# Turned rows by TensorE transposes instead of DMA transposes, and late row pairs folded by VectorE

## The chip, the cores and the metric

The kernel runs on one core of one Trainium2 chip. The metric is the device time of the program in microseconds (us), as the median of several runs; lower is better. Names of engines: PE is TensorE (PEld its weight loads), DVE is VectorE, ACT is ScalarE, POOL is GpSimd, and SP is SyncE, which here only issues DMAs.

## The reference, cut to what matters

Four layers are applied to `x` of 2048 rows by 512 columns, a spectral layer (A) and a mixing MLP (B) in turn, twice, each on the normalised rows and added to `x`:

```python
def _A_ref(x, w_r, w_i):
    X = rfft2(x)
    X = X * (w_r + 1j * w_i)
    return irfft2(X, s=(S, D)).astype(bfloat16)

def _B_ref(x, w1, w2, w3, w4):            # w1, w2: 512x512; w3: 512x1792; w4: 1792x512
    h = _gelu(_layernorm(x) @ w1)
    # quarters of h's columns shifted by +1, -1, +2, -2 rows
    hs = concatenate([g0, g1, g2, g3]) @ w2
    x1 = x + hs
    return x1 + _gelu(_layernorm(x1) @ w3) @ w4

x = A_x
x = x + _A_ref(_layernorm(x), A_w_r, A_w_i)
x = x + _B_ref(_layernorm(x), B_w1, B_w2, B_w3, B_w4)
x = x + _A_ref(_layernorm(x), A_w_r, A_w_i)
x = x + _B_ref(_layernorm(x), B_w1, B_w2, B_w3, B_w4)
```

## The kernel before

The whole state `x_state` stays in SBUF as 128 partitions by 16 row blocks `q` by 512 columns; row `16 p + q` lies in partition `p`. The kernel calls `layer` twice; one `layer` is one spectral layer and the MLP behind it.

The spectral layer is a chain of small matmuls. A Fourier transform over `p` (`front`) gives `V`; then over the columns (`over_d`), over `q` (`over_q`), the product with the filter `W` (`weigh`, which writes `PB`), and back over `q` (`back_q`), over the columns (`back_d`, letters D and C, with the table `G`) and over `p` (`back_p`, letter P, with the table `Tinv`). Between two of them ACT or DVE copies the result out of PSUM. `back_d` of a pair `m` of row blocks leaves two halves in PSUM, an even and an odd part of the columns. `take_D` (letter Y) copies both to SBUF as `Y`, and `back_p` then makes each half of the 512 columns from both parts with two accumulating matmuls: four matmuls of 256 columns for each row block. `half_D` and `fold_D` (letters K and H) are a second way that the code holds: ACT or DVE copies the odd half to SBUF, DVE writes the sum and the difference of the parts as `Y`, and `back_p` then needs only two matmuls. The constant `FOLD` lists for which `m` the second way is taken; before, for none.

In the MLP, rows must be turned before the products with `w1` and `w3`, so that columns lie on the partitions. `norm2` and `norm3` write normalised rows to `xn`, and `turn` turns two row blocks, 128x1024, with one DMA transpose from SP to the tile `xT`: letter T before `w1` (function `tr`), letter U before `w3` (`tr3`); eight of each in a layer. `w1` (letter v) and `w3` (letter w) multiply, `gelu1` (h) and `gelu3` (g) on ACT take the results out; `w2` (letter u), `add_x1` (f), `w4` (letter W) and `add_x2` (A) end the MLP. The statistics of the norms are letters s and k on ACT.

The program is scheduled by hand. Three strings, `ORDER_0` for the first `front`, `ORDER_A` and `ORDER_B` for the two calls of `layer`, name every operation in the order in which it is issued; each engine works through its own operations in that order. A last letter A, V, P or D says which engine does an operation that could run on several, and a number behind a dot says which of the eight PSUM banks it writes:

```python
    for op in (ORDER_B if last else ORDER_A).split():
        op, _, bank = op.partition(".")
        K.bank = int(bank) if bank else None
        if op[0] == "X":
            fill(K, int(op[1:]))
            continue
```

SP's queue carries, in this order: `x`, the filter `W` in four groups (`load_W`), then, after a small copy `gate2` that waits until the last part of `W` is in place, `G`, `Tinv`, `w1`, `w2`, `w3`; a dummy transpose; the transposes, with `w4` issued behind the eighth of the first layer; and at the end the stores. POOL's queue carries the tables `FL`, `TL`, `TR`, and four copies W to W that double the filter. ACT's queue carries the table `T` and one column of each of the two planes of `W`. `fill` issues matmuls on zeros.

Of the kernel before, what the change touches and what calls it, by code (L numbers as in the profile page):

```python
# [13 lines left out]
BF16 = dt.bfloat16  # L14
FP32 = dt.float32

P = 128
# [11 lines left out]
def dft_tables():  # L29
# [12 lines left out]
    p = np.arange(P)  # L42
    pair = lambda j, s: (j if s == 0 else 64 - j) if j else 32 * s
    T = np.zeros((P, NH, 2, 2))
    for j in range(NH):
        for s in range(2):
            i = pair(j, s)
            T[:, j, s, 0] = np.cos(2 * np.pi * i * p / 128)
            T[:, j, s, 1] = np.sin(2 * np.pi * i * p / 128) if i else np.cos(np.pi * p)
    T = T.reshape(P, P)  # L50
    d = np.arange(D // 2)
    f = np.arange(1, 257)
# [9 lines left out]
    w = np.full(256, 2.0)  # L62
    w[255] = 1.0
    G = np.stack([cos * w, sin * w]) / (S * D)
    G = G.transpose(2, 0, 1).reshape(2, P, 2, D // 2).transpose(1, 0, 2, 3)
    A = np.zeros((NH, NQ, 2, 2, 2, 32))
    B = np.zeros((NH, NQ, 2, 2, 2, 32))
    q = np.arange(NQ)
    for j in range(NH):
        for sg in range(2):  # L70
            for m in range(32):
                k = 64 * m + (j if sg == 0 else 64 - j if j else 32)
# [24 lines left out]
           "Tinv": np.stack([T.T, -T.T], axis=1)}  # L97
# [43 lines left out]
def banks(K, n):  # L141

    k = K.bank
    if k is None:
        k = K.next_bank if K.next_bank + n <= 8 else 0
        K.next_bank = (k + n) % 8
    return K.ps[:, k:k + n, :]


def copy(K, dst, src, eng):  # L150
    if eng == "V":
        K.nc.vector.tensor_copy(dst, src)  # L152
    else:
        K.nc.scalar.activation(dst, src, ACT.Copy, bias=0.0, scale=1.0)  # L154


def load_all(K, A_x, A_w_r, A_w_i, B_w1, B_w2, B_w3, B_w4):
# [16 lines left out]
    for pl, v in enumerate(planes):  # L174
        nc.scalar.dma_start(K.W[2::4, pl, 0], v[:, 32])
    for lo in range(0, NH, 8):
        for pl, v in enumerate(planes):
            load_W(K, v, pl, lo, lo + 8)
    K.TL = K.const.tile([P, 2, NB, P], BF16, name="TL")
# [28 lines left out]
    def load_mlp():  # L208
        gate2 = K.const.tile([1, 16], BF16, name="gate2")
        nc.sync.dma_start(gate2[:], K.W[1:2, 1, NH - 1, 1:17])  # L210
        for k in ("G", "Tinv"):
            table(k, nc.sync)
        for k, w, n, c in (("w1", B_w1, 4, D), ("w2", B_w2, 4, D), ("w3", B_w3, 4, FH), ("w4", B_w4, 14, D)):
            t = K.const.tile([P, n, c], BF16, name=k)
            setattr(K, k, t)
            if k != "w4":
                load_halves(t, w, n)

    def load_w4():
        load_halves(K.w4, B_w4, 14)  # L220

    def load_halves(t, w, n):
        v = w.rearrange("(t p) n -> p t n", p=P)
        for part in (slice(0, n // 2), slice(n // 2, n)):
            nc.sync.dma_start(t[:, part], v[:, part])

    K.load_w4 = load_w4
# [10 lines left out]
def load_W(K, v, pl, lo, hi):  # L238


    j1 = max(lo, 1)
    fwd, rev = [K.W[2 * sg::4, pl] for sg in range(2)]
    K.nc.sync.dma_start(fwd[:, lo:hi], v[:, lo:hi])
    K.nc.sync.dma_start(rev[:, j1:hi], v[:, 65 - hi:65 - j1][:, ::-1])
# [243 lines left out]
def first_front(K):  # L488
# [66 lines left out]
    dummy = K.const.tile([P, 1, P], BF16, name="dummy")  # L555
    K.nc.sync.dma_start_transpose(dummy[:], K.zeros[:])
# [11 lines left out]
def layer(K, last):  # L568
# [144 lines left out]
    def turn(to, k, rows):  # L713

        g, h = divmod(k, 2)
        if g not in to:
            to[g] = K.grp.tile([P, 4, 4, P], BF16, name="xT", bufs=4)
        nc.sync.dma_start_transpose(to[g][:, 2 * h:2 * h + 2].rearrange("p q t c -> p (q t) c"),
                                    rows.rearrange("p q d -> p (q d)"))

    def tr(k):
        turn(xT, k, xn[:, 2 * k:2 * k + 2, :])
        turned.append(k)
        if len(turned) == 8 and not last:
            K.load_w4()
# [48 lines left out]
    def tr3(k):  # L774
        q = ROWS[2 * k]
        turn(xT3, k, xn[:, q:q + 2, :])
# [84 lines left out]
    def act_table(k):  # L861
# [4 lines left out]
    next_V, turned = {}, []  # L866
    table = {"z": act_table, "e": lambda g: ln[g].std_twice(), "i": lambda g: ln[g].invert_twice(), "M": lambda g: ln[g].shift(), "J": invert4, "d": over_d, "t": take_d, "q": over_q, "x": take_q, "p": weigh, "b": lambda b: back_q(b, first_half(b)), "V": lambda b: back_q(b, 1),
             "D": lambda m: back_d(m, 0), "C": lambda m: back_d(m, 1), "Y": take_D, "P": back_p, "a": add_x, "s": stats2, "r": rstd2, "c": lambda g: ln[g].ratio(), "n": norm2,
             "T": tr, "v": w1, "h": gelu1, "u": w2, "f": add_x1, "k": square3, "E": resid,
# [34 lines left out]
FLEX = "mlGLnotxYIKEpQ"  # L904
FOLD = [(), ()]
ORDER_0 = """
s1 f0 s0 s3 s2 i3 i2 i0 s4 s5 S1 J1 s7 S0 J0 s6 i7 f2 Q2A Q3A i4 Q0A s9 i6 s8 O1.2 s11 f3 S2 J2 Q6P Q1A Q5A O0.4 i8
G1A Q4V O2.0 s10 i11 i10 S3 Q7P O3.2 G0A s13 J3 Q10V Q11A s12 s14 i12 O5.6 i14 G3A i13 G2A Q8P Q9P s15 S4 J4 O4.4 G5A
i15 Q12V Q13V S5 O6.0 L5A J5 Q14P O7.6 G4A G6A G3V Q15V L6V G7A O8.0 L7A G8A I3V L8A
"""  # L910
ORDER_A = """
d0.3 t0A d2.4 d1.2 d4.0 q0.6 t1V N0 t2A q1.2 d6.4 t4A q2.0 x1V x0V p1V t6A q4.2 d12.6 d10.4 x2A p2P p0V t12A t10A d8.0
p4D b0.6 d14.7 q10.4 m0V q6.2 t8A x10A t14A b1.0 b5.1 m5A m1A q12.4 q14.6 p6D b4.1 b2.0 p10V x14A p14P d15.2 m4A m2A
t15A q8.6 x8A b3.1 b7.0 m7A b11.2 q15.6 m11A x15A b10.3 b14.0 m3A b6.2 m6A p12D V12.4 b12.5 p8V p15V b13.7 b9.1 m10A
m12A b8.6 b15.2 m13V V15.3 m14V m9A m8V V13.5 V14.0 m15A D1.6 l12V D0.1 l15A l13A l14V C1 C0 Y0V Y1A D3.3 C3 P3.0 a3
P2.6 Y3A a2 s3 P0.5 a0 s2 P1.2 a1 s0 D2.0 C2 Y2V s1 r0 D5.6 C5 P7.2 a7 Y5A e0 s7 P6.4 D7.0 P4.5 a6 i0 M0 P5.2 D4.6 C4
P10.3 s6 C7 n2P a4 s4 a5 n3V n0V s5 Y4A D6.4 r1 P11.2 C6 P8.6 P9.7 e1 n1V a10 T1 Y7A P15.0 i1 M1 n5A s10 n4P n6P P14.1
Y6V P13.3 a8 s8 T0 a9 n7P s9 a11 P12.4 a15 s11 v1.6 r2 n10P T2 h1 T3 a13 a12 n11V c0 s15 T5 n8V v0.2 h0 s13 v3.4 n9V
v2.2 h3 u0.0 s12 h2 u1.4 a14 c1 s14 T4 u3.1 r3 f0 k0 n14V v5.2 n13A n15V T7 f1 E1V h5 f3 v4.6 u2.0 f2 E2V h4 c2 u6.6
f6 u5.5 f5 E5V k3 E6V n12P u7.0 E0V u4.1 f4 T6 v7.5 k2 k1 R0 E3V o2V o1V h7 o3A c3 v6.1 h6 o0P f7 u8.0 f8 E8P u13.5  # L920
u12.2 u11.6 u14.3 U1 f12 k4 k5 k7 f14 E14V k12 k6 u9.2 f11 u10.4 k8 E7V f13 k13 f10 R1 o7P o5P u15.3 E10V U0 w4.0 E4P
f9 E9P k11 f15 w2.4 g2 k10 o4V U2 w1.2 k14 g4 E15P k9 E13P w3.6 g3 g1 w5.0 w0.4 g0 w6.6 g5 g6 E11V W1.2 o6P U3 E12V A1
W3.6 A3 B3 B1 w8.0 W2.4 A2 W0.2 k15 R2 o10P o11A R3 o14V o9A g8 o12A w13.0 U5 w7.6 B2 g13 o8P U4 w15.4 w10.0 A0 B0 g10
w16.2 j1 g7 g16 w18.0 g18 w9.2 o15P w11.0 g9 w12.2 g12 j3 w17.6 j2 j0 S0 Q3V Q1V Q2P Q0V g11 W4.2 U7 O1.0 o13P g17 U6
A4 W7.3 B4 j4 G1A G1V A7 B7 j7 O0.0 w19.6 G0A W6.2 A6 g19 W5.3 A5 g15 B5 w23.4 g23 j5 B6 j6 S1 Q4P G0V w27.2 g27 I0V
w14.6 g14 Q5V O2.0 w20.2 w24.6 g20 W10.2 A10 B10 Q7V j10 W8.3 G2A A8 B8 W9.4 A9 B9 Q6V j9 W11.2 A11 w26.4 I1P B11 j11
g24 j8 O3.2 w22.6 S2 Q10P g26 G2V I2P Q11A Q8P g22 w21.0 g21 G3A w25.6 G3V g25 W12.0 A12 B12 j12 Q9P S12 J12 I3P O4.5
G4A Q12A G4V W15.1 A15 I4P B15 j15 W13.2 A13 S15 J15 B13 j13 W14.3 Q15P W24.2 S13 J13 Q13P O5.0 A14 A24 B14 B24 j14
G5A O15.4 G15V O6.2 S14 J14 L15A Q14A O14.4 G6A L6A G14A G5V I5V L14A
"""  # L930
ORDER_B = """
X6.7 d4.4 d15.7 t15A d12.2 t4V d1.0 d0.1 q15.4 t1V q4.6 t12A x15V q1.2 t0A x4A d2.0 p15P p1D q0.4 p0D q12.6 d10.2 t2A
x12A d8.0 q2.4 d6.6 t10A b1.3 p4V b5.2 t8A t6A q8.0 m1A m5A q6.6 p12P p2D x6A q10.3 b0.2 x10A b3.5 b2.6 m2A b4.7 m4A
d14.4 t14A p8D b9.1 m9A b13.0 p6V b12.3 p10V b7.6 m13A m7A m0A b6.4 q14.0 b15.7 b10.6 m3V b8.2 b11.5 m15A p14D b14.7
m12A m8V m14V V12.0 V14.1 V15.3 V13.2 m10A m6A l14V m11A l12A D2.5 l15V l13A D3.0 C3 Y3A C2 D1.2 C1 Y2V Y1A P7.1 a7
P6.0 a6 P4.5 P5.7 P2.2 P3.3 D0.0 s7 a4 s6 C0 a5 D5.4 s4 s5 r1 C5 a3 s3 Y0V D6.6 a2 e1 P0.0 P1.2 i1 a0 a1 Y5A P10.1 M1
n4V n5P D4.4 C4 P11.0 s2 T2 s0 n7V n6V T3 s1 r0 a10 a11 Y4A C6 e0 i0 D7.2 C7 P9.1 Y6A M0 n0P P8.4 Y7A P12.0 s11 n1V T0
a8 s10 P13.5 a9 s9 n3V n2P T1 c0 P15.2 a15 s8 P14.3 a14 s15 r2 n11V v3.1 h3 v2.3 h2 v0.6 h0 n10P T5 v1.2 a13 s13 n8P
h1 u0.4 s14 n9V T4 u3.5 a12 c1 u1.0 s12 r3 f3 u2.7 f1 k1 n14V n15P T7 f0 v5.2 c3 f2 v4.0 n13A h5 u4.3 n12V T6 f4 E3V
k0 h4 E1V u6.7 c2 u7.6 f7 k3 E0V u5.1 k2 R0 E7V E2V o1P o2P f5 E5V k4 v6.5 h6 o0A v7.0 h7 u13.6 o3V U1 u12.4 u15.5 f6  # L940
E6P f13 E13P u14.3 f14 k7 k5 E14V k6 R1 o7A E4V u11.0 f15 f12 k14 k12 u9.2 E15P f9 k13 o6V u8.1 u10.3 f10 E10V f11
E11V k15 U0 w6.4 w4.2 g4 k9 f8 E8V R3 o15A E12V o13V k10 w5.0 w1.2 g5 o12P k11 g1 w2.6 w0.1 g2 o14V g0 k8 R2 o11V o8P
w3.6 U3 g3 o5A U6 U7 w26.0 w21.2 g21 w22.6 g26 w23.2 E9V o9P g6 W0.0 A0 o4V U2 W3.1 W2.0 g23 g22 w25.2 W1.4 g25 w11.2
g11 o10V w27.6 g27 w8.2 g8 U4 w12.6 A3 A1 w24.4 w10.2 A2 w7.0 g10 g24 W12.2 W14.3 y3 y0 A14 A12 w9.4 g9 W13.2 A13 U5
w13.4 g13 y2 w15.2 W15.4 g7 y1 A15 g12 y12 W6.7 g15 A6 w16.0 g16 y13 W5.2 w17.4 g17 w14.0 g14 w20.4 w18.0 y6 y14 g20
g18 W7.6 A7 y7 W4.4 A5 A4 y4 y5 w19.6 g19 y15 W9.1 A9 W8.3 y9 W11.0 A11 y11 W10.5 W20.4 A8 y8 A10 y10 A20 y20
# [31 lines left out]
```

## Time and profile before

| what | value |
|---|---|
| median of 3 runs | 343.75 us (343.66 to 343.83) |
| the profiled execution's own time | 343.63 us |
| its span, first to last instruction | 341.8 us |
| granted TensorE clock | 1.000 |
| PE busy | 334.3 us, 98% of the span |
| PEld, DVE, ACT, POOL busy | 186.8, 163.5, 192.0, 117.5 us |
| DMA transposes xT<-xn | 32, median 3.1 us from issue to landing |

The layout of the span, by the trace: the first `front` matmul starts at 8.2 us, the first `over_d` at 19.0, `back_d` at 36.8, `w1` at 51.2 us, `w3` from 79 us; the second layer's `over_d` starts at about 182 us, `back_d` at 199.4, `w1` at 214.6 and `w3` at about 242 us. The last matmul ends at 339.1 us.

Busy time of PE is a union over matmuls whose ends are modelled: a matmul of 512 columns is shown with 379 ns although the next one starts 216 ns later. What one costs in a stream is therefore read from a run of equal ones: its length divided by its count.

### The profile page before, as it was taken

How to read it: one execution, taken by the hardware profiler on the slowest of the kernel's cores; microseconds unless marked ns; L12 is line 12 of the kernel's file. 1: busy time of each engine (PE TensorE's matmuls, PEld its weight loads, DVE VectorE, ACT ScalarE, POOL GpSimd, SP SyncE). 2: the span in 40 equal slices, each digit the busy share in tenths (PEclk: the TensorE clock that was granted, in tenths of full speed). 3: DMA queues.
4: the chain of work that ended last, by engine and by line, in shares of the span. 5: the costliest groups of instructions: out<-in, count | busy, mean ns of one | idle time of the engine just before them, and what ended most of it. 6: DMA issues, size and time to landing. Idle time of an engine off the chain costs nothing.

```text
span 341.8 us, 5734 instructions
## 1 busy us (share of the span) xinstructions
PE 334.3 (98%) x2184; PEld 186.8 (55%) x2184; DVE 163.5 (48%) x373; ACT 192.0 (56%) x356; POOL 117.5 (34%) x218
## 2 busy tenths in 40 slices
PE   6999999999999999999999999999999999999996
PEld 4878984444444444444467898444444444444443
DVE  4979895659034023535378979456901110200112
ACT  6989899665821542421628979986695132142310
POOL 3795067669633000402432505877722000000000
PEclk9999999999999999999999999999999999999999
DMA  7985936390231100000000003543130500000011
GB/s 261 313 284 197 339 78 117 71 270 19 46 61 31 32 0 0 2 0 0 2 0 2 2 3 64 104 83 61 33 61 0 125 31 0 15 17 32 15 63 46
DMA packets 45340, 24.60 MB, mean 72 GB/s; under 512 B 35153, under 2 KB 42321, under 8 KB 45313
## 3 DMA queue, kind: packets, MB, share of 16 engines
q1 hardware_dynamic: 43824, 19.74, 23.0%
q0 software_dynamic: 1248, 4.40, 3.9%
q8 instruction: 17, 0.28, 0.3%
q10 hardware_dynamic: 240, 0.10, 0.1%
q14 instruction: 11, 0.08, 0.1%
HBM read 11.61 MB, written 2.10 MB: 40 GB/s over the span
## 4 chain that ended last, share of the span: by engine, by line
PE 85%; ACT 8%; DVE 3%; DMA 2%; issue 1%; SPq 0%; ACTq 0%
PE ps L804 28%; PE ps L784 28%; PE ps L749 8%; PE ps L733 6%; PE ps L642 4%; ACT xn L303 3%; PE ps L612 2%; PE ps L594 2%; DVE x_state L698 2%; PE ps L662 2%; DMA x_state<-in_A_x_dram 1%; ACT hT L740 1%; DMA xT<-xn 1%; PE ps L439 1%; PE ps L429 1%
## 5 line engine op out<-in xcount | busy, mean ns | idle before, releaser
L791 ACT ACTIVATE gT<-ps 128x1024 bf16<-128x1024 f32 x56 | 55.7, 1023 | 97.6 <-PE ps L784 95.5
L804 PE MATMUL ps<-w,gT 128*128 128x512 bf16 (+2 forms) x476 | 99.4, 366 | 0.0
L784 PE MATMUL ps<-xT,w 128*128 128x512 bf16 x448 | 99.3, 379 | 0.0
L810 DVE TENSOR_TENSOR x_state<-ps,x_state 128x512 bf16<-128x512 f32 (+2 forms) x34 | 22.1, 659 | 123.4 <-PE ps L804 123.1
L804 PEld LDWEIGHTS <-gT 128*128 128x128 bf16 x476 | 45.4, 98 | 51.4
L784 PEld LDWEIGHTS <-w 128*128 128x128 bf16 x448 | 43.7, 98 | 52.1
L757 DVE SCALAR_TENSOR_TENSOR xn<-xn,ln_c,ps 128x512 bf16<-128x512 bf16 x32 | 23.3, 742 | 16.0 <-PE ps L749 6.3
L733 PE MATMUL ps<-xT,w 128*128 128x512 bf16 x128 | 28.6, 379 | 0.4 <-DMA xT<-xn 0.4
L749 PE MATMUL ps<-w,hT 128*128 128x512 bf16 x128 | 28.8, 379 | 0.1
L326 POOL TENSOR_SCALAR ln_ve<-ln_mv 128x4 f32<-128x4 f32 x11 | 3.0, 271 | 57.7 <-DVE ln_mv L319 57.0
L303 ACT ACTIVATE junk<-xn 128x512 bf16<-128x512 bf16 x32 | 19.8, 623 | 5.0 <-DVE xn L757 5.0
L291 DVE BATCH_NORM_STATS2 ln_st<-x_state 128x6 f32<-128x512 bf16 (+2 forms) x30 | 19.5, 665 | 3.5 <-DMA x_state<-in_A_x_dram 3.0
L698 DVE SCALAR_TENSOR_TENSOR x_state<-ps,x_state 128x512 bf16<-128x512 f32 x32 | 20.6, 684 | 0.9 <-PE ps L690 0.9
L733 PEld LDWEIGHTS <-w 128*128 128x128 bf16 x128 | 12.4, 98 | 15.6 <-DMA xT<-xn 1.0
L749 PEld LDWEIGHTS <-hT 128*128 128x128 bf16 x128 | 12.5, 98 | 15.4 <-ACT hT L740 1.0
L303 ACT ACTIVATE xn<-x_state 128x512 bf16<-128x512 bf16 x32 | 19.9, 626 | 0.8 <-DVE x_state L698 0.8
L740 ACT ACTIVATE hT<-ps 128x512 bf16<-128x512 f32 x32 | 17.6, 600 | 4.6 <-PE ps L733 4.5
L690 PE MATMUL ps<-Y,Tinv 128*128 128x256 bf16 x128 | 15.8, 272 | 0.4 <-DVE Y L152 0.4
L631 POOL TENSOR_TENSOR PB<-X,W 128x2048 bf16<-128x2048 bf16 (+1 forms) x4 | 12.1, 3033 | 11.2 <-DVE X L152 7.3
L154 ACT ACTIVATE TV<-ps 128x1024 bf16<-128x1024 f32 (+1 forms) x17 | 14.6, 895 | 2.4 <-PE ps L594 2.3
L642 PE MATMUL ps<-TR,PB 128*128 128x128 bf16 x256 | 15.9, 219 | 0.0
L662 PE MATMUL ps<-G,hT 128*128 128x256 bf16 x128 | 15.6, 273 | 0.0
(96 smaller groups left out, 414.0 us busy)
## 6 DMA issues: line engine op xcount, KB each, us to landing
w<-in_B_w_dram SPq DMA_DIRECT2D x4, 896.0 KB, 7.0
W<-W POOLq DMA_DIRECT2D x4, 514.0 KB, 5.1
x_state<-in_A_x_dram SPq DMA_DIRECT2D x8, 256.0 KB, 4.9
out_dram<-x_state SPq DMA_DIRECT2D x15, 128.0 KB, 1.8
w<-in_B_w_dram SPq DMA_DIRECT2D x4, 256.0 KB, 4.4
W<-in_A_w_r_dram SPq DMA_DIRECT2D x7, 128.5 KB, 5.4
W<-in_A_w_i_dram SPq DMA_DIRECT2D x7, 128.5 KB, 5.6
TL<-tab_TL POOLq DMA_DIRECT2D x3, 256.0 KB, 5.5
```

What stands on the lines that cost most here:

```text
L303: K.nc.scalar.activation(out, src, ACT.Square, bias=0.0, scale=D ** -0.5, accum_out=self.s[:, i, 1:2])
L642: nc.tensor.matmul(o[:, k0 * P:(k0 + 1) * P], lhsT=pab[u][:, k, 2 * (b - u) + h, f * P:(f + 1) * P], rhs=K.TR[:, k:k + 2, 2 * b + h], star ...
L662: nc.tensor.matmul(o[:, i, e * 256:(e + 1) * 256], lhsT=M[:, F, e, 2 * m + i, :], rhs=K.G[:, F, e, :], start=(F == 0 and e == 0), stop=(F ...
L698: nc.vector.scalar_tensor_tensor(K.x[:, q, :], ps.pop(("P", q)), 1.0, K.x[:, q, :], op0=ALU.mult, op1=ALU.add, accum_out=ln[g].s[:, i, 0:1])
L733: nc.tensor.matmul(o[:, i], lhsT=K.w1[:, t, j * P:(j + 1) * P], rhs=xT[g][:, :, t, :], start=(t == 0), stop=(t == 3))
L740: nc.scalar.activation(hv[:, 2 * h + i, 4 * g:4 * g + 4, PAD:PAD + P], o[:, i].rearrange("p (q c) -> p q c", q=4), ACT.Gelu_apprx_tanh, bi ...
L749: nc.tensor.matmul(o, lhsT=K.hT[:, j, st:st + P], rhs=K.w2[:, j, :], start=(j == 0), stop=(j == 3))
L757: nc.vector.scalar_tensor_tensor(xn[:, q, :], xn[:, q, :], ln[q // 4].c[:, q % 4:q % 4 + 1], ps.pop(("u", n)), op0=ALU.mult, op1=ALU.add, ...
L784: nc.tensor.matmul(o[:, i], lhsT=K.w3[:, c, t * P:(t + 1) * P], rhs=xT3[g][:, :, c, :], start=(c == 0), stop=(c == 3))
L791: nc.scalar.activation(gT[g][:, 2 * j:2 * j + 2, :], ps.pop(("w", k)), ACT.Gelu_apprx_tanh, bias=0.0, scale=1.0)
L804: nc.tensor.matmul(o, lhsT=gT[g][:, t, i * P:(i + 1) * P], rhs=K.w4[:, t, d], start=(t == 0), stop=(t == 13))
L810: nc.vector.tensor_tensor(x, ps.pop(("W", n)), x, op=ALU.add)
```

## The change

Four things are changed together.

1. `turn` no longer issues a DMA transpose. It issues eight TensorE transposes of 128x128 against a unit matrix, into one PSUM bank read as bf16, and a new operation `take_turned` copies the 128x1024 result to `xT` on ACT or DVE (letters Z behind T and F behind U).
2. `FOLD` lists the row pairs 4 to 7 in both layers.
3. Loads: the unit matrix is loaded on SP behind `Tinv`; `w4` is loaded with the other weights, not behind the eighth transpose; the two column loads of `W` go from ACT's queue to SP's, behind the first group of `W`; the dummy transpose goes.
4. All three orders are new.

```diff
-           "Tinv": np.stack([T.T, -T.T], axis=1)}
+           "Tinv": np.stack([T.T, -T.T], axis=1), "unit": np.eye(P)}
...
-    for pl, v in enumerate(planes):
-        nc.scalar.dma_start(K.W[2::4, pl, 0], v[:, 32])
     for lo in range(0, NH, 8):
         for pl, v in enumerate(planes):
             load_W(K, v, pl, lo, lo + 8)
+        if lo == 0:
+            for pl, v in enumerate(planes):
+                nc.sync.dma_start(K.W[2::4, pl, 0], v[:, 32])
...
-        for k in ("G", "Tinv"):
+        for k in ("G", "Tinv", "unit"):
             table(k, nc.sync)
...
-            if k != "w4":
-                load_halves(t, w, n)
+            load_halves(t, w, n)
...
-    dummy = K.const.tile([P, 1, P], BF16, name="dummy")
-    K.nc.sync.dma_start_transpose(dummy[:], K.zeros[:])
...
-    def turn(to, k, rows):
-
-        g, h = divmod(k, 2)
+    def turn(key, rows):
+
+        ps[key] = o = banks(K, 1)[:, 0].bitcast(BF16).rearrange("p (i t c) -> p i t c", i=2, t=4)
+        for i in range(2):
+            for t in range(4):
+                nc.tensor.transpose(o[:, i, t], rows[:, i, t * P:(t + 1) * P], K.unit[:])
+
+    def take_turned(to, key, eng):
+        g, h = divmod(key[1], 2)
         if g not in to:
             to[g] = K.grp.tile([P, 4, 4, P], BF16, name="xT", bufs=4)
-        nc.sync.dma_start_transpose(to[g][:, 2 * h:2 * h + 2].rearrange("p q t c -> p (q t) c"),
-                                    rows.rearrange("p q d -> p (q d)"))
+        copy(K, to[g][:, 2 * h:2 * h + 2], ps.pop(key), eng)
...
-FOLD = [(), ()]
+FOLD = [(4, 5, 6, 7), (4, 5, 6, 7)]
 ORDER_0 = """
-s1 f0 s0 s3 s2 i3 i2 i0 s4 s5 S1 J1 s7 S0 J0 s6 i7 f2 Q2A Q3A i4 Q0A s9 i6 s8 O1.2 s11 f3 S2 J2 Q6P Q1A Q5A O0.4 i8
+s0 s2 s1 f0 s3 i2 s5 f2 i0 S0 i3 S1 s7 J0 s6 Q0A s4 s9 J1 Q1V O0.5 Q2A i6 i4 i7 S2 s10 J2 Q3A s11 f3 Q4A Q5A s8 i11
...
 ORDER_A = """
...
-P10.3 s6 C7 n2P a4 s4 a5 n3V n0V s5 Y4A D6.4 r1 P11.2 C6 P8.6 P9.7 e1 n1V a10 T1 Y7A P15.0 i1 M1 n5A s10 n4P n6P P14.1
-Y6V P13.3 a8 s8 T0 a9 n7P s9 a11 P12.4 a15 s11 v1.6 r2 n10P T2 h1 T3 a13 a12 n11V c0 s15 T5 n8V v0.2 h0 s13 v3.4 n9V
-v2.2 h3 u0.0 s12 h2 u1.4 a14 c1 s14 T4 u3.1 r3 f0 k0 n14V v5.2 n13A n15V T7 f1 E1V h5 f3 v4.6 u2.0 f2 E2V h4 c2 u6.6
+Y2V Y3A P3.1 P2.3 P7.4 a0 s0 a1 s1 P6.0 a3 s3 D5.6 C5 P4.1 a2 s2 K5A P5.5 D4.2 a6 s6 a7 a4 r0 e0 a5 C4 s7 K4A i0 M0
+n2P n3A s4 D6.4 D7.0 C7 n0P H5 H4 n1V s5 T1.6 Z1A r1 e1 P11.7 P8.2 T0.3 a11 i1 M1 n4P a8 Z0A C6 P10.6 P9.7 n6A v1.2 h1
+a9 n5P T2.7 a10 n7P T3.6 s11 v0.2 K6V H6 Z3V P12.6 Z2A v3.4 K7V c1 c0 s9 P13.7 H7 P15.0 P14.1 s10 s8 h3 h0 r2 v2.4 n9P
...
```

By the two programs' instructions, PE gains 256 transposes (8 turns of each kind in each of 2 layers, 8 transposes each) and loses 32 of its 128 matmuls of `back_p`; every other kind of matmul has the same count. ACT and DVE gain 32 copies of 128x1024. SP's queue holds no transpose any more. The six zero matmuls that opened `ORDER_B` (`X6.7`) stand in front of `P10` now (`X6.2`). In the spectral stage the filter products that POOL did in `ORDER_A` and `ORDER_B` (`p2P p14P` and `p15P p12P`) are on DVE.

## The prediction

> **What bounds the kernel now.** I read the share of busy time first, then the slices, the chain in order of time, the groups by form and what PE waited for.
>
> The page, parts 1 and 2 (busy us, share of the span, instructions; then tenths in 40 slices):
>
> ```profile
> PE 334.3 (98%) x2184; PEld 186.8 (55%) x2184; DVE 163.5 (48%) x373; ACT 192.0 (56%) x356; POOL 117.5 (34%) x218
> ...
> PE   6999999999999999999999999999999999999996
> ...
> PEclk9999999999999999999999999999999999999999
> ```
>
> PE is busy in every slice at full clock. But ends of matmuls are modelled, so I need what a matmul costs in an unbroken stream. The chain of what ended last (start, length, work) gives it:
>
> ```profile
> 72.33 6.91 PE ps L749 x32
> 125.43 0.45 PE ps L439 x8
> 199.53 2.62 PE ps L662 x24
> ```
>
> 6.91/32 = 216 ns for 512 columns, 2.62/24 = 109 ns for 256, 0.45/8 = 56 ns for 128. The second row matters most: each of those eight matmuls has its own 128x128 weights and 128 columns, the shape of a turn.
>
> Now the sum over all matmuls of before, counts from the groups by form: 1124 of 512 columns x 0.216 = 242.8; 28 of 384 (three quarters of 0.216, an estimate) 4.6; 392 of 256 x 0.109 = 42.7; 476 of 128 x 0.056 = 26.7; 128 of L612 at about 0.06 (16 took 0.98 in the chain) 7.8; six zero matmuls 0.7. Together 325.3 us. PE runs from the first front matmul at 8.2 us to 339.1 us, 330.9 us. So all of PE's slack after the head is about **5.6 us**, and PE is the bound nearly everywhere. What the waits name of it is small:
>
> ```profile
> PE ps L429 <- ACT Tq L412: 2.4, 2, 1.9
> ...
> PE ps L733 <- DMA xT<-xn: 0.4, 2, 0.3
> PE ps L690 <- DVE Y L152: 0.4, 1, 0.4
> PE ps L588 <- DVE V L471: 0.3, 1, 0.3
> ```
>
> Only 0.4 us of PE's waiting is for a DMA transpose: what the change removes is nearly hidden already.
>
> One stage is tight on three engines, the end of the spectral layer (busy us and counts of PE, PEld, DVE, ACT, POOL, then clock, DMA share, GB/s):
>
> ```profile
> 40.00:50.00 10.00, 10.00 (x94) 8.93 (x93) 9.61 (x27) 9.84 (x24) 4.39 (x13) 1.00 0.50 150
> 50.00:60.00 10.00, 9.74 (x50) 4.51 (x48) 6.01 (x19) 9.95 (x25) 7.57 (x18) 1.00 0.62 117
> ```
>
> The new evictions come just there.
>
> **The change part by part.** The profiled execution took 343.63 us (span 341.8, 1.8 around it), 0.12 under the median; I take that as equal.
>
> *Transposes on PE.* 256 of them. No transpose is in the trace. Nearest row: 56 ns, the 128-column matmul with its own weights (L439; L642 gives 3.68/64 = 58 in the chain). 256 x 0.056 = **+14.3 us**, all on the path because PE has no idle time to put them in. Two rules of the Trainium skill ("TensorE: Matmul & The Clock Gate") speak for more. "Back-to-back issue gap" says that streams in which every matmul has its own weight load sustain about 81 ns at 128 columns: 20.7 us, 6.4 more. The trace has such streams at 56 to 58, so I do not use 81. "Part 4: PE-mode transpose" gives about 275 ns for a transpose in a kernel, and says that the full clock does not engage for transposes: 70.4 us by that, 56 more. But a single 128-column matmul here is also shown with 219 ns of length while the stream advances by 56, so I read 275 as a length, not a period. And a turn is a burst of 8, 0.45 us, between long matmul streams, so the granted clock should stay 1.00. I take 56. Bounds: 32 turns may each cost a change into and out of the transposing mode; the largest regular step at a change of kind in the trace is the one out of the half-array matmuls L612, 142 ns by the starts. 64 x 0.142 = 9.1 us above, none below. Below 56 I know no row; 128 columns must stream.
>
> *Fold.* 4 pairs x 2 rows x 2 layers = 16 rows, each two matmuls of 256 columns fewer: 32 x 0.109 = **-3.5 us** of PE, on the path.
>
> *DMA transposes gone.* -0.4 us, the wait shown. Their queue is SP's; nothing else waited behind it. The first turned tile comes sooner (0.45 + one copy of 1.0 to 1.2 against a median of 3.1 us to landing), but there PE was busy with other work anyway.
>
> *Evictions.* 32 copies of 128x1024, 19 on ACT and 13 on DVE by the letters of the orders. These rows bound them:
>
> ```profile
> L154 ACT ACTIVATE Y<-ps 128x1024 bf16<-128x1024 f32 x11 | 11.1, 1015 | 2.6 <-PE ps L662 1.4 <-issue 1.1
> ...
> L152 DVE CAST Y<-ps 128x1024 bf16<-128x1024 f32 x5 | 6.1, 1223 | 3.1 <-PE ps L662 3.0
> ...
> L152 DVE CAST hT<-ps 128x512 bf16<-128x512 f32 x4 | 2.7, 687 | 0.0
> ```
>
> ACT: 19 x 1.0 = 19 us. DVE: by the row of f32, 13 x 1.22 = 16 us. The skill ("VectorE: DVE Perf Modes", "Why PSUM operands drop a tier") says that a PSUM operand still allows two elements a cycle for 16-bit data; from 687 and 1223 ns (slope 1.05 ns an element, 0.15 fixed) that makes 0.15 + 0.54 = 0.69 us, 9 us in all. Not shown here: I take 1.22 for the sum, 0.69 as the lower bound. Half of the copies (U) lie in the stage of w3 and w4, where ACT idled 95.5 us for L784 alone: nothing, hidden by PE's own stream. The other half (T) lie in the tight stage.
>
> *The tight stage, layer A, from the first back_d to the first w2.* What each engine must do there, by the orders and the advance from start to start (Y 0.9 on ACT, a row's square with its read 0.64, a gelu pair 0.98, table load 1.3):
> - PE before: back_d 64 x 0.109 = 7.0, back_p 64 x 0.109 = 7.0, four w1 of 8 x 0.216 = 6.9; 20.9. After: 7.0 + 5.2 + 6.9 + four turns 1.8 = 20.9.
> - ACT before: 5 Y, 15 squares, 4 gelu pairs, a table load, two small roots 0.5, a norm 0.7: about 20.2. After: 3 Y, 2 half_D of 0.5, 12 squares, 2 norms, 3 Z, the rest equal: about 21.0.
> - DVE before: 3 Y, 15 row sums of 0.65, 5 norms of 0.4: about 15.5. After: one Y, 4 folds of about 1.3, 2 half_D of 0.69, 15 row sums, a Z, 3 norms: about 20.
>
> So ACT passes PE by a little and DVE comes level; with three engines level, hand-overs will show on PE. I charge ACT's growth, 0.8 us a layer: **+1.6 us**. Bounds: nothing if squares slip behind, as ACT has room from 60 us on; 3 us a layer if DVE's chain row sum, norm, turn, copy is late.
>
> *Spectral stage.* POOL's four filter products go to DVE, 1.9 us a layer more; DVE had 8.68 and 8.41 of 10 us between 20 and 40 us, so it is covered by DVE's own gaps; if not, up to 1 us a layer. The same for POOL's gain: nobody waited for POOL there.
>
> *Loads.* ACT's queue loses two issues (0.63 and 0.61 us at 1.1 us). ACT's first work starts at 3.9 us, with the landing of x, so nothing. SP gets them behind the first group of W: later issues slip by 1.2 us, but between 10 and 20 us the DMA share is 1.00, so landings follow the bandwidth, not the issue. Behind them hang POOL's doubling copies, gate2 and G: G was issued at 31.86, 2.8 us to landing, first back_d at 36.8, so 2 us of cover against 1.2. Cost 0; if the cover is gone, at most 1. unit: 32 KB between Tinv and w1, needed 10 us later. w4 earlier: no transposes compete any more, w4 is needed at 91 us; nothing. The dummy: nothing.
>
> *New orders.* The head (front, up to 19.0 us) has the same sums: ACT 17.5 us both times, DVE 16.7 and 17.3. I take 0, bounds -1 and +1. The zero matmuls moved to before P10 in the second layer mean that PE is expected to wait there: 0 net.
>
> Sum: 343.6 + 14.3 - 3.5 - 0.4 + 1.6 = **355.6 us**.
>
> **The rivals.**
> 1. *Additive, as above*: 0.72. 352.5 (slack smaller than now by 2) to 358.5.
> 2. *Transposes cost more than a matmul of their size*: a step at every burst, or 81 ns. +6.4 to +9.1: 362 to 364.7. Against: L439 and L642. For: no trace shows the mode. 0.14. The extreme of 275 ns, 411 us, I leave out.
> 3. *The evictions bind*: ACT and DVE late in the tight stage, PE waits 3 us a layer rather than 0.8: 360. For: 9.84 and 9.61 of 10 us above. Against: room from 60 us on, and the orders mix T, Z and w1 among the last back_p. 0.12.
> 4. *Faster than before*: only if a transpose costs far less than 56 ns. Its place is the 32 bursts. With the 0.4 and 3.5 saved, and no charge for the tight stage, the break-even is 3.9/256 = 15 ns; at 10 ns it would be 342.3. Taking every microsecond of slack (5.6) by better orders does not do it at 56 ns: 343.6 + 10.8 - 5.6 = 348.8. 0.02, which I share with no change.
>
> **How the numbers follow.** About 0.2% (0.7 us) can be told from no change by this measurement. Slower by more: all of cases 1 to 3, 0.98. The likeliest is case 1, 355.6. The range leaves out the upper part of case 2 and what lies below 352.5: 352.5 to 361.5.
>
> **What would show it.** Right: PE's 256 new instructions advance by 56 ns in a burst; P loses 32; span about 353.8; PE's share still 98%; granted clock 1.00; no wait of w1 or w3 for a copy above 1 us in all. Rival 2: starts in a burst over 60 ns apart, or a gap over 0.1 us at its edges. Rival 3: PE waits for xT from ACT or DVE, or for Y, of 2 us or more in 36 to 62 and in the same stage of the second layer. The forecast is wrong if the span grows by less than 8 or more than 18 us.

## The result, and the profile after

The changed kernel takes **357.92 us** (four runs, 357.71 to 358.13) against 343.71 us of before on the same occasion: 1.0413 times as long, 95% interval 1.0395 to 1.0431. That is 14.2 us more; 11.9 were forecast, and the time lies inside the range given. The profiled execution of after took 357.88 us, span 356.1; its span is 14.3 us longer than that of before.

The page of after, PE's share and the slices:

```profile
PE 347.6 (98%) x2408; PEld 198.5 (56%) x2408; DVE 181.6 (51%) x399; ACT 208.7 (59%) x381; POOL 102.7 (29%) x213
...
PE   7989989999999999999999999999999999999996
...
PEclk9999999999999999999999999999999999999999
```

PE's share and the clock are what they were; PE simply has more to do, and two slices, one at the start of the first spectral stage and one at the end of that layer, are no longer full. The chain that ended last, in order of time, at the end of the first spectral layer:

```profile
42.70 4.03 DVE x_state L691 x14
...
47.15 0.67 DVE Y L670 x2
...
48.24 1.28 DVE Y L670 x2
...
50.78 0.92 ACT xT L154
51.74 1.89 PE ps L728 x8
53.62 0.89 PE ps L711 x16
```

The last row holds the disputed price: 16 transposes in 0.89 us, 56 ns each. Nor does a change into or out of the transposes cost anything: by the starts in this trace PE enters and leaves 23 unbroken bursts of them, and at 44 of these 46 edges the step is that of the stream within 1 ns; at the other two PE loses 0.22 and 0.33 us. The rows above show where the chain left PE: up to 51.7 us it runs through DVE's row sums (L691) and folds (L670) and a copy of turned rows on ACT, then returns to PE with `w1` (L728 here). Before, it ran through ACT in this stage of layer A. In layer B it already ran through DVE's row sums before the change, and from there through a DMA transpose to `w1`:

```profile
211.02 3.50 DMA xT<-xn
```

After the change it runs there through row sums and folds on DVE. The new rows among the groups by form:

```profile
L154 ACT ACTIVATE xT<-ps 128x1024 bf16<-128x1024 bf16 x19 | 19.0, 1019 | 12.4 <-PE ps L711 12.4
L711 PE MATMUL ps<-unit,xn 128*128 128x128 bf16 x256 | 18.2, 219 | 0.5 <-ACT xn L397 0.3 <-DVE xn L395 0.2
L670 DVE TENSOR_TENSOR Y<-ps,half 128x512 bf16<-128x512 f32 x16 | 10.0, 679 | 0.1
L152 DVE COPY xT<-ps 128x1024 bf16<-128x1024 bf16 x13 | 8.9, 687 | 11.4 <-PE ps L711 11.3
```

A transpose is shown with the same length, 219 ns, as a matmul of its size. ACT's copy from bf16 costs what one from f32 cost (1019 against 1015 ns), DVE's far less (687 against 1223).

To see where the 14.3 us of span lie, I cut both traces at the first matmul of a stage. "Lost" is the stage's length less its matmuls at 216, 162, 109 and 56 ns (before rounding, 215.8 and 55.8; a half-array one at 56), zero matmuls counted as lost.

| stage, from first matmul to the next stage's first | before, us (lost) | after, us (lost) | change in lost |
|---|---|---|---|
| start to first front | 8.23 | 8.48 | +0.25 |
| first front | 10.73 (1.05) | 10.50 (0.81) | -0.24 |
| spectral, layer A | 17.89 (1.89) | 18.89 (2.89) | +1.00 |
| back_d to w1, layer A | 14.31 (0.36) | 13.86 (1.62) | +1.26 |
| w1 to w3, layer A | 27.92 (0.29) | 28.68 (0.05) | -0.24 |
| w3 to next over_d | 103.00 (0.96) | 108.80 (0.62) | -0.34 |
| spectral, layer B | 17.28 (1.28) | 18.12 (2.12) | +0.84 |
| back_d to w1, layer B | 15.21 (1.26) | 13.89 (1.66) | +0.40 |
| w1 to the last matmul | 124.31 (0.0) | 131.42 (0.0) | 0.0 |
| last matmul's start to the end | 2.92 | 3.44 | +0.52 |

PE's matmuls themselves make 256 x 0.056 - 32 x 0.109 = 10.85 us; the last column makes 3.45; together 14.3. The six zero matmuls of layer B (0.65 us) leave the row from `w3` to the next `over_d` and enter the row from `back_d` to `w1` of layer B. Without them these two rows would read +0.31 and -0.25.

### The profile page after: what moved, and what is told of

The parts are those of the page before. It is cut to its first block, busy times and chain, and to the rows that moved or that the text cites. A ratio compares the mean times of both kernels' runs of the same rounds, so it can differ in the third digit from the quotient of the medians.

```text
span 356.1 us, 6134 instructions
## 1 busy us (share of the span) xinstructions
PE 347.6 (98%) x2408; PEld 198.5 (56%) x2408; DVE 181.6 (51%) x399; ACT 208.7 (59%) x381; POOL 102.7 (29%) x213
## 4 chain that ended last, share of the span: by engine, by line
PE 88%; DVE 5%; ACT 3%; issue 1%; DMA 1%; SPq 0%; ACTq 0%; DVEq 0%
PE ps L799 27%; PE ps L779 27%; PE ps L728 8%; PE ps L744 8%; PE ps L635 4%; PE ps L711 4%; DVE x_state L691 3%; PE ps L424 3%; PE ps L655 2%; PE ps L587 1%; PE ps L605 1%; DMA x_state<-in_A_x_dram 1%; DVE Y L670 1%; ACT TV L154 1%; PE ps L434 1%
## 5 line engine op out<-in xcount | busy, mean ns | idle before, releaser
L744 PE MATMUL ps<-w,hT 128*128 128x512 bf16 x128 | 30.6, 379 | 0.0
L728 PE MATMUL ps<-xT,w 128*128 128x512 bf16 x128 | 29.4, 379 | 0.5 <-ACT xT L154 0.5
L154 ACT ACTIVATE xT<-ps 128x1024 bf16<-128x1024 bf16 x19 | 19.0, 1019 | 12.4 <-PE ps L711 12.4
L691 DVE SCALAR_TENSOR_TENSOR x_state<-ps,x_state 128x512 bf16<-128x512 f32 x32 | 20.5, 684 | 3.0 <-PE ps L678 1.5
L728 PEld LDWEIGHTS <-w 128*128 128x128 bf16 x128 | 12.4, 98 | 14.4 <-issue 0.7
L304 POOL TENSOR_SCALAR ln_mv<-ln_s 128x4 f32<-128x4 f32 x16 | 4.1, 258 | 55.8 <-DVE x_state L691 49.1
L711 PEld LDWEIGHTS <-xn 128*128 128x128 bf16 x256 | 16.1, 98 | 5.6 <-ACT xn L397 0.6
L711 PE MATMUL ps<-unit,xn 128*128 128x128 bf16 x256 | 18.2, 219 | 0.5 <-ACT xn L397 0.3
L621 DVE TENSOR_TENSOR PB<-ps,W 128x1024 bf16<-128x1024 f32 x15 | 17.7, 1216 | 0.0
```

Of the source, the lines that this page charges most:

```text
L691: nc.vector.scalar_tensor_tensor(K.x[:, q, :], ps.pop(("P", q)), 1.0, K.x[:, q, :], op0=ALU.mult, op1=ALU.add, accum_out=ln[g].s[:, i, 0:1])
L711: nc.tensor.transpose(o[:, i, t], rows[:, i, t * P:(t + 1) * P], K.unit[:])
L728: nc.tensor.matmul(o[:, i], lhsT=K.w1[:, t, j * P:(j + 1) * P], rhs=xT[g][:, :, t, :], start=(t == 0), stop=(t == 3))
L744: nc.tensor.matmul(o, lhsT=K.hT[:, j, st:st + P], rhs=K.w2[:, j, :], start=(j == 0), stop=(j == 3))
```

## The experiments

These are twelve kernels, measured on three occasions on which before took 344.07, 343.42 and 343.78 us; differences from the changed kernel's 357.9 of less than about 0.7 us are therefore read only where the trace shows them in one place.

**Each transpose issued twice (e3).**

```diff
-            for t in range(4):
+            for t in (0, 0, 1, 1, 2, 2, 3, 3):
```

> The changed kernel with every one of the 256 transposes issued twice, to the same place: 256 more instructions on PE and nothing else. Theory of the prediction (PE is the bound, a transpose in a stream costs 56 ns, as a matmul of 128 columns does): 256 x 0.056 = 14.3 us more, 372.2 us. Rival, that a transpose costs more than its size says (81 ns): 378.6 us. Rival, that turns partly lie in idle time of PE or that only the edges of a burst cost: below 368 us.

371.10 us, ratio 1.0776 [1.0745, 1.0807]: 13.2 us more. The chain of this run:

```profile
48.59 1.05 PE ps L711 x16
50.12 0.91 PE ps L711 x16
54.01 1.79 PE ps L711 x32
```

32 in 1.79 us are 56 ns again. The stages show 14.3 us more of PE's work and less lost between back_d and w1 (1.62 to 0.95 and 1.66 to 1.15, zero matmuls counted): part of the doubled transposes stood where PE waited. The price of 56 ns is settled; 81 ns would have been 378.6. The edges of a burst are not doubled here: that they cost nothing is read from the steps in after.

**Without the fold (f1).**

```diff
-FOLD = [(4, 5, 6, 7), (4, 5, 6, 7)]
+FOLD = [(), ()]
 # and in both orders K4 to K7 become Y4 to Y7 on the same engine, H4 to H7 drop out
```

> The changed kernel without the fold: pairs 4 to 7 are copied whole again (take_D where half_D stood, on the same engine), fold_D drops out, back_p has 128 matmuls; the rest of the order stays. Theory of the prediction (the fold saves 3.5 us on the path): 357.9 + 3.5 = 361.4 us. Rival, that DVE's chain of row sums and folds sets the end of the spectral layer (PE lost 1.6 us there in the first layer), so that the fold gives back part of what it saves: PE's loss between the first back_d and the first w1 falls below 0.6 us in each layer and the time is 358.5 to 360 us.

361.50 us, ratio 1.0522 [1.0506, 1.0538]: 3.6 us more, the full price of 32 matmuls. PE still loses 1.60 and 1.89 us between back_d and w1. The rival falls: the folds stood in the chain there, but without them the chain goes through ACT instead, with about the same loss. Its rows in this run:

```profile
42.80 2.28 ACT xn L298 x7
...
45.35 0.91 ACT Y L154
...
47.67 0.91 ACT Y L154
...
50.51 0.91 ACT xT L154
...
51.60 0.92 ACT xT L154
```

**The copies before w1 done twice (f3).**

```diff
-        copy(K, to[g][:, 2 * h:2 * h + 2], ps.pop(key), eng)
+        o = ps.pop(key)
+        for _ in range(2 if key[0] == "T" else 1):
+            copy(K, to[g][:, 2 * h:2 * h + 2], o, eng)
```

> The changed kernel with each copy of turned rows before w1 (16 of them, Z) done twice: ACT and DVE get 16 x 1.0 or 0.69 us more, in the tight stage; PE gets nothing. If the evictions hold PE there: each layer's first w1 comes 1 to 2 us later, and the gelus, 2 to 4 us in all: 360 to 362 us. If only DVE's row sums and folds bind there: up to 0.9 us a layer, the second copy ahead of the first w1: 358 to 359.5 us.

367.92 us, ratio 1.0698 [1.0672, 1.0724]: 10.0 us more, beyond both expectations. By the trace 9 of the copies are on ACT and 7 on DVE, 9 x 1.02 + 7 x 0.69 = 14.0 us of work, of which ten come out in the time. PE lost 3.73 us from back_d to w1 in layer A and 3.16 from w1 to w3 (1.62 and 0.05 in after), 3.77 and 2.95 in layer B. A part of this is not waiting but the clock, which fell behind the waits in both layers:

```profile
56.00:60.00 4.00, 4.00 (x27) 2.61 (x26) 1.41 (x4) 3.54 (x7) 2.38 (x7) 0.72 0.00 0
228.00:232.00 4.00, 3.15 (x8) 1.17 (x8) 2.63 (x6) 3.95 (x10) 1.97 (x5) 0.61 0.00 0
```

By the starts, some 7 us of the loss are waits and some 3 us matmuls at half clock; the one of the five runs whose mean clock was 1.00 took 366.17 us, 8.3 more than after. So the copies before `w1` have little cover. Whether the load of ACT and DVE counts here, or only that each xT comes later, this run doesn't separate.

**The copies before w3 done twice (f5).** The same edit for "U".

> The changed kernel with each copy of turned rows before w3 (16 of them, F) done twice. The prediction put these copies at nothing, hidden by PE's own stream: 357.9 us, within 0.5. If ACT and DVE are short there too, as the run with the copies before w1 doubled showed for that stage (+10 us): 361 us or more.

361.72 us, ratio 1.0520 [1.0506, 1.0534]: 3.8 us more, the rival's side. PE's waits name the place:

```profile
PE ps L781 <- ACT xT L154: 3.1, 3, 1.1
```

L781 is `w3` there. One wait stands at the first `w3` of layer A, whose turns end 1.7 us of matmuls ahead of it: by the trace the second ACT copy is what it waits for. The other two lie amid `w3` and `w4` (at 112.5 and 276.4 us), the first of them behind four ACT copies in a row. As they are, these copies cost nothing (0.62 us lost in the stage of w3 and w4 against 0.96 before); but the cover is short, not the 95.5 us of idle ACT that I had named.

**All copies before w1 on DVE (f6).**

```diff
 # nine letters of ORDER_A and ORDER_B: Z1A -> Z1V, Z0A -> Z0V, Z2A -> Z2V, ...
```

> The changed kernel with all copies of turned rows before w1 on DVE: nine move from ACT, where one takes 1.02 us, to DVE, where one takes 0.69. If ACT binds the tight stage (squares, gelus, copies): 1 to 2 us less, 356 to 357 us. If DVE does (row sums, folds): 359 to 362 us.

363.91 us, ratio 1.0583 [1.0568, 1.0597]: 6.0 us more, although the sum over both engines falls (9 x 0.33 = 3 us less). PE waits for DVE now:

```profile
PE ps L728 <- DVE xT L152: 4.3, 4, 1.8
```

The profiled execution, 1.05 us above the median, also lost 1.1 us in the first front; from the first over_d on, the trace is 5.9 us longer than that of after, which is the six. So in this order DVE has no room for these nine copies.

**The filter products back on POOL (f4).**

```diff
 # ORDER_A: p2V -> p2P, p14V -> p14P; ORDER_B: p15V -> p15P, p12V -> p12P
```

> The changed kernel with four filter products back on POOL where the order of before had them there (units 2 and 14 in the first layer, 15 and 12 in the second), at their new places in the order. If DVE's load is why PE lost 2.9 us rather than 1.9 in the first spectral stage: 357.9 - 1.0 = 356.9 us, at best 356. If the place in the order counts (POOL takes 2 to 4 us where DVE takes 0.7 to 1.2): the same or slower, 358 to 360 us.

358.47 us, ratio 1.0434 [1.0418, 1.0450]. By the time alone not told apart from after; the trace loses 3.08 and 2.61 us in the two spectral stages, against 2.89 and 2.12. So moving the products back to POOL at these places gains nothing; in layer B PE then waits 0.7 us for one of POOL's products (by the starts). In layer A a larger part of the loss is named by the waits of after:

```profile
PE ps L583 <- DVE V L152: 0.8, 1, 0.8
```

That is the second group of `over_d`, at 20.0 us, for a copy of `V` that DVE makes at the end of the first front in the new order. By the starts PE stands 0.99 us there, in this run as in after, and 0.28 us in before. It comes ahead of all filter products.

**The spectral orders of before (e4).**

```diff
 # ORDER_0 of before; in ORDER_A and ORDER_B all operations ahead of the first back_d in before's order,
 # engines and banks (without X6.7); the rest as changed
```

> The changed kernel with the order of before in the first front and in both spectral stages up to the first back_d (the filter products of POOL included), and the new order from there on. In the trace of after PE lost 2.9 and 2.1 us there, against 1.9 and 1.3 before. If the new order of that stage, with POOL's products moved to DVE, is the cause: 357.9 - 1.8 = 356.1 us. If the cause is the work behind it (evictions of turned rows holding ACT and DVE), no change: 357.9.

357.34 us, ratio 1.0394 [1.0353, 1.0435], an interval that takes in after. By the trace layer A's spectral stage lost 2.22 us (2.89 after, 1.89 before) and layer B's 2.26 (2.12 and 1.28). So two thirds of the added loss in layer A come with the new order: the wait for `V` is 0.28 us again. But the first front loses 0.3 us more than in after, so that of the 0.8 us that both stages together had lost only 0.4 come back. In layer B the old order wins nothing: it loses 0.63 us at a new place, the first `back_d`, for an ACT copy of hT. What the loss in layer B comes from stays open.

**DMA turns under the new orders (e1).**

```diff
-                nc.tensor.transpose(o[:, i, t], rows[:, i, t * P:(t + 1) * P], K.unit[:])
+        nc.sync.dma_start_transpose(to[g][:, 2 * h:2 * h + 2].rearrange("p q t c -> p (q t) c"),
+                                    rows.rearrange("p q d -> p (q d)"))
 # take_turned does nothing
```

> The changed kernel with the turns done by DMA transposes again: no transposes on PE, no copies of turned rows on ACT and DVE; fold, loads and orders stay new. Additive theory: 357.9 - 14.3 = 343.6 us, plus what the later landing costs where the new order puts w1 and w3 only 1 to 2 us of PE work behind the turn and a DMA transpose takes 3.1 us: 1 to 2 us at two places of each MLP half, together some 5: 348 us (345 to 351). Rival, that the copies of turned rows are what costs, beside PE: below 343 us, as ACT and DVE are 28 us lighter.

359.24 us, ratio 1.0452 [1.0392, 1.0511]: both theories missed, by 11 and by 16 us. 14.3 us of PE's work and 28 us of copies are gone and the time is that of after. PE lost 4.6, 5.0, 4.4 and 5.0 us in the two stages of each layer from back_d to w3:

```profile
PE ps L727 <- DMA xT<-xn: 6.9, 4, 2.9
PE ps L727 <- DVE xn L395: 2.2, 1, 2.2
...
PE ps L678 <- DVE Y L670: 1.1, 2, 0.8
```

With 1.0 and 0.7 us in two smaller rows these waits are about 12 us, where I had expected 5. And more is lost than these waits. The stretches 48 to 52 and 52 to 56 us:

```profile
48.00:52.00 4.00, 1.84 (x14) 1.01 (x12) 3.73 (x12) 2.74 (x8) 2.80 (x8) 1.00 1.19 222
52.00:56.00 4.00, 2.43 (x6) 0.87 (x7) 3.93 (x8) 1.64 (x2) 3.67 (x7) 0.60 0.78 147
```

PE was busy 1.84 of 4 us in the first; in the second the granted clock is 0.60. By the starts the first matmuls of `w1` behind the wait stand 427 ns apart instead of 216, in layer B as well; over both layers that is some 4 us. So I had sized the waits at less than half and had not counted the clock. The run says what DMA transposes cost in an order made for the other way, not what they cost in before.

**The fold alone, in the kernel before (e2).**

```diff
-FOLD = [(), ()]
+FOLD = [(4, 5, 6, 7), (4, 5, 6, 7)]
 # ORDER_A: Y5A -> K5A, with H5 behind a6; Y4A -> K4A H4; Y7A -> K7A H7; Y6V -> K6V H6
 # ORDER_B: Y5A -> K5A H5; Y4A -> K4A H4; Y6A -> K6A H6; Y7A -> K7A H7
```

> The kernel before with the fold alone: pairs 4 to 7 of both layers as half_D and fold_D in the place of take_D, orders otherwise as before, turns by DMA. Additive theory: 32 matmuls of 109 ns fewer on PE, -3.5 us, against DVE's extra work of about 5 us a layer in a stage where DVE had some gaps: 343.7 - 3.5 + 1.6 = 341.8 us (340.2 to 344). Rival, that DVE becomes the bound at the end of the spectral layer, as the chain of after shows there: 344 us or more.

353.75 us, ratio 1.0278 [1.0245, 1.0312]: ten slower than before instead of two faster, as the rival had it and more. PE's waits, and three stretches:

```profile
PE ps L685 <- DVE Y L677: 6.4, 8, 1.5
```

```profile
48.00:52.00 4.00, 1.96 (x17) 1.27 (x14) 3.38 (x9) 1.80 (x5) 0.85 (x4) 1.00 0.37 70
52.00:56.00 4.00, 2.40 (x10) 1.21 (x11) 3.90 (x10) 2.26 (x6) 2.45 (x4) 0.66 0.62 115
56.00:60.00 4.00, 4.00 (x11) 1.50 (x10) 2.92 (x11) 3.97 (x9) 2.83 (x8) 0.50 0.40 77
```

`back_p` waits for folds that stand behind other work on DVE (3.90 of 4 us busy), eight times in the two layers; then the clock falls to half, and only 11 matmuls start in the last 4 us.

**The same with zero matmuls in the waits (f2).**

```diff
 # eight operations X8 (eight zero matmuls of 256 columns each) ahead of rows of back_p:
 # ORDER_A ahead of P10, P8, P15, P13; ORDER_B ahead of P10, P9, P12, P13
```

> The kernel before with the fold alone, as in the run that took 353.75 us, and eight zero matmuls put in front of seven or eight back_p rows of pairs 4 to 7 in all, where PE waited for Y. In that run the granted clock was 0.66 and 0.50 between 52 and 60 us, behind 4 us in which PE was half idle. If the clock is a part of its loss, the fillers keep it at 1.00, the first 16 matmuls of w1 in the first layer run at 216 ns and the time falls by 4 to 6 us, to 348 to 350 us, although 6 us of matmuls are added. If the wait for DVE is all, nothing is gained: 353.7 us or more. A third outcome, that fillers push back_p and so the rows: above 355.

351.74 us, ratio 1.0249 [1.0226, 1.0272]: 2.0 us less than without them, with 64 matmuls (7.0 us) more. The same stretches:

```profile
48.00:52.00 4.00, 3.82 (x36) 3.18 (x34) 3.38 (x8) 1.60 (x5) 0.65 (x3) 1.00 0.43 82
52.00:56.00 4.00, 3.55 (x27) 2.35 (x25) 3.90 (x10) 2.46 (x6) 2.45 (x4) 1.00 0.61 113
56.00:60.00 4.00, 4.00 (x21) 1.82 (x19) 2.92 (x11) 3.97 (x10) 3.04 (x8) 1.00 0.35 67
```

The clock stays at 1.00 and 21 matmuls start where 11 did. The stage from back_d to w1 takes 18.04 us in layer A both times: the fillers fit into the waits exactly. So about 2 of e2's 10 us were the clock, less than I expected. The rest is the waits for DVE: they go on, with zero matmuls in them.

**Turns before w3 by DMA, those before w1 by PE (f8).**

```diff
-        turn(("U", k), xn[:, q:q + 2, :])
+        nc.sync.dma_start_transpose(to[g][:, 2 * h:2 * h + 2].rearrange("p q t c -> p (q t) c"),
+                                    rows.rearrange("p q d -> p (q d)"))
 # take_turned copies only for "T"
```

> The changed kernel with the turns before w3 done by DMA again (no transposes on PE and no copies for them), those before w1 by PE. PE has 128 transposes fewer: 357.9 - 7.2 = 350.7 us if the DMA's 3.1 us to landing is covered; the new order leaves 1.7 us of PE work between the second turn and the first w3, so 1 to 2 us of wait in each layer: 352.5 us (350.7 to 355).

355.48 us, ratio 1.0333 [1.0313, 1.0354]: 2.4 us faster than after, but three slower than expected. In its profiled execution the first over_d comes at 22.19 us (18.99 in after), because the third of the eight loads of x landed 0.8 us later (6.96 us against 6.15), and because the clock then fell:

```profile
4.00:8.00 4.00, 2.43 (x17) 1.83 (x16) 2.48 (x7) 2.35 (x7) 0.82 (x4) 1.00 0.99 347
8.00:12.00 4.00, 2.70 (x17) 2.14 (x17) 3.69 (x13) 3.95 (x14) 3.29 (x8) 0.56 0.83 259
12.00:16.00 4.00, 4.00 (x32) 3.27 (x30) 3.86 (x14) 2.10 (x5) 2.05 (x4) 0.59 0.90 284
```

From the first over_d to the last matmul it takes 4.7 us less than after: 7.2 of transposes, less 2.0 of one wait for a DMA and 0.5 in small pieces. With the 0.5 us by which its end is shorter, the step itself makes 5.2 us, close to the 5.4 expected. The mean clock of its four runs, 0.990 to 0.995 against 1.000, suggests that all of them lost something there; why x lands later in this kernel is not shown. None of the twelve is faster than the kernel before, and none puts the turns on PE alone into the order of before.

**More instructions on SP (f7).**

```diff
     K.load_mlp()
+    for k in range(32):
+        K.nc.sync.dma_start(spare[:, k:k + 1], K.zeros[0:1, k:k + 1])
```

> The changed kernel with 32 copies of one element each on SP's queue behind the weights' loads, long before the stores. In after the end of the program, from the last matmul to the last instruction, takes 3.2 us against 2.7 before; SP's closing drain starts 0.4 us later than its last wait would let it. If that hangs on how many instructions SP's program holds (33 DMA transposes fewer): the end takes 2.7 us again and the time is 357.4. If not: 357.9.

356.94 us, ratio 1.0385 [1.0371, 1.0399]. The end of the program takes 2.94 us from the last matmul's start, as before, not 3.44: SP's closing drain no longer starts late. The two runs with DMA transposes on SP under the new order, e1 and f8, end in 2.94 and 2.92 us as well; the others made from the changed kernel end in 3.44 to 3.47. So the 0.5 us at the end hang on SP's program, from which the change takes 33 DMA transposes, and not on the stores. Which property of it, its length or where it ends, isn't shown.

## Why the prediction was right, step by step

- **What bounds the kernel**: right. PE stayed at 98%, and 10.85 of the 14.3 us are PE's own work, the sum of the next two terms.
- **Transposes, +14.3**: right, 56 ns each in after and in e3, and nothing at the edges. Of the two figures of the Trainium skill ("TensorE: Matmul & The Clock Gate") that were weighed, 81 ns ("Back-to-back issue gap") and 275 ns ("Part 4: PE-mode transpose"), neither is the step in these bursts; the granted clock stayed at 1.00. The matmul with its own weights was the right row to read.
- **Fold, -3.5 on the path**: right in the changed kernel (f1: 3.6), but I had added it as if it belonged to the fold alone. e2 shows that, put where the plain copies stood in the order of before, it costs ten. What in the new order makes the folds come in time was not tested piece by piece.
- **DMA wait, -0.4**: gone, as said, but it was larger: by the starts 0.32 us in layer A and 0.45 in layer B, since the view of waits counts from a matmul's modelled end. In layer A a wait for ACT's copy took its place (0.63 us by the starts).
- **Evictions**: the half before w3 cost nothing, as said, with less cover than I named. For DVE I took 1.22 us from the f32 row; it is 0.687. The lower bound, 0.69 by the Trainium skill ("VectorE: DVE Perf Modes", "Why PSUM operands drop a tier": two 16-bit elements a cycle even from PSUM), was the right one. The sum did not move by it, since it had charged ACT's growth alone.
- **The tight stage, +1.6 (with the DMA wait, +1.2)**: the table has +1.26 and +0.40, together 1.66, but the agreement is luck. I had charged both layers alike. Layer A carries it; in layer B the waits fell by 0.25 us, and the rest is the moved zero matmuls. My own terms for ACT, added again, make 20.5 and 21.5 us, a growth of 1.0 and not 0.8. And the engine was not the one charged: the chain goes mainly through DVE, which I had at 20 of 20.9 us; ACT has only its last 1.2 us. That three engines come close was right: without the folds the chain goes through ACT (f1), and DVE can't take ACT's copies (f6).
- **Spectral stage and new orders, 0**: the mis-sized terms. The spectral stages lost 1.00 and 0.84 us more, and the way into the second one 0.31. I had looked at the one thing named there, POOL's products. My bound of 1 us a layer holds, but for another reason: 0.71 us of layer A's loss is the wait for `V` at the end of the first front, a thing of the new order. Layer B's stays open.
- **The end, not in my sum**: +0.52 us, tied by f7 to SP's program.
- **Head, loads**: +0.25 and -0.24, inside the bounds.

The miss of 2.3 us is thus 2.15 in and around the spectral stages and 0.5 at the end, less 0.4 in the tight stage and behind it.

## What to carry to other kernels

Where one engine is busy from end to end, work moved to it from an idle queue is paid nearly in full (13.2 of 14.3 us in e3), however cheap each piece is: take the price from the stream of the most similar instruction, and multiply. What the moved work then needs on other engines (here the copies) is judged by the reserve of the stage that it falls in, and idle time summed over the whole kernel says nothing about that. A saving such as the fold's belongs to an order as much as to the operation (3.6 us won in one, ten lost in the other): measure it in the order that is meant to use it.

## What the runs showed of the hardware

- The granted TensorE clock falls to half behind some stretches in which PE idles. The means of 0.56 to 0.72 above are mixtures: by the clock's own records it was 0.50 from 53.3 to 60.1 us in e2, 52.8 to 56.2 in e1, 54.8 to 58.2 in f3, 8.5 to 15.3 in the head of f8, and 1.00 around them. All eight such stretches of these traces last 3.4 or 6.8 us. In them matmuls of 512 columns stand 427 ns apart, so that a wait can cost a second time.
- No single wait of e2 or f3 was longer than 1.7 us by the starts, half of the gaps of some 3.4 us that the Trainium skill ("TensorE: Matmul & The Clock Gate", "HAM oscillation") warns of: here several shorter ones came together, with PE 49% busy for 4 us in e2. Zero matmuls in these waits held the clock at 1.00 at no cost in time (f2). But no rule for it comes out of these runs: f6 had waits of 1.05 and 1.93 us close together around 225 us, e1 one of 2.4 at 68 us, and the clock stayed at 1.00. So did it in after, where the longest wait, in the head, is 1.3 us.
- In the head the same holds. By the starts PE stood idle between its zero matmuls and the first front matmul 1.3 us in after, 2.1 in before, 2.3 in f6, 2.9 in e3 and 3.0 in f8. The clock fell in f6 and f8 and not in e3, so the length of the wait alone doesn't decide. In f8 the head took 3.2 us longer in all, though x had landed only 0.8 us later.
- DVE copies 128x1024 from PSUM in 0.69 us where both sides are bf16, against 1.22 us from f32; ACT takes 1.02 us for either.
